# Gated block attention with a Fourier mixer on one core: the keys of nine head pairs turned by DMA transposes instead of TensorE

## The chip, the cores and the metric

The kernel runs on one core of a Trainium2 chip. The metric is the device time of one execution in microseconds (us). The engines are named as the profile names them: PE (TensorE), DVE (VectorE), ACT (ScalarE), POOL (GpSimd) and SP (SyncE, which here only issues DMAs).

## The reference

Inputs q, k and v have 4 batches, 8 heads, 768 positions and 64 dimensions. The output has 4 x 768 x 512 elements in float32.

```python
# attention: every query sees its own block of 64 keys and the three blocks with the best gate
k_rep  = k.reshape(B, H, 12, 64, D).mean(axis=3)
gate   = einsum('bhsd,bhnd->bhsn', q, k_rep)          # blocks ahead of the query's own: -1e9
mask   = (block in top 3 of gate, or own block) and key <= query
attn   = softmax(where(mask, q @ k.T / 8, -1e9)) @ v
x      = attn, heads side by side                     # (4, 768, 512)
# mixer and perceptron
u  = x + real(fft(fft(x, axis=1), axis=2))
un = (u - mean(u)) / sqrt(var(u) + 1e-6)
out = u + relu(un @ w_ch1) @ w_ch2                    # w_ch1 512 x 2048, w_ch2 2048 x 512
```

## The kernel before

The work is cut into 16 head pairs P (batch b = P // 4, two heads each), and for each batch into a Fourier step and a perceptron. Every step is a small function with a two-letter name, and a string `ORDER` lists all steps as `name:arguments`. Each engine, SP and POOL included, takes its own instructions in the order of that string; semaphores do the rest. So the order is fixed in advance, and it interleaves the perceptron of one batch with the attention of the next.

The steps of one pair:

- `Lk`, `Lq`, `Lv`: loads of keys, queries and values as they stand in memory (position on the partition), issued by SP (`load`, lines 270 and 275).
- `tk`, `tq`: six TensorE transposes each, of 128 x 128 float32, to put the dimension on the partition (line 292).
- `ks`: DVE sums the turned keys over each block of 64 (line 297); `kh` halves the result by head.
- `kc`: ACT copies the turned keys from PSUM into the tile `qk` in float16 (line 308, or 311 in two halves). `qc` and `qs` do the same for the queries by DVE and POOL.
- `g`, `gt`, `gx`, `gl`, `gm`: gate scores on PE, then transposes, top three and the mask on DVE. `K` (POOL, eight small selects) writes the mask into rows 64 to 95 of `qk`.
- `s`: six tiles of scores on PE, `e`: their exponentials on ACT, `d`: the causal select on POOL, `vc`: the cast of v on POOL, `v`: scores times v on PE, `x`: division on DVE.

The first seven pairs (P < `NX` = 7) add the mask by extra matmuls. The last nine pairs hold it inside the product: `qk` has 96 rows, 64 of the dimension and 32 that pair the mask on the query side with a 0/1 table of blocks (`ind`) on the key side. That table is loaded once into each of the three `qk` slots (`Lc`, `Li`).

For a batch: `fs`, `fd`, `f` (folds on DVE), `y` and `m` (Fourier products on PE), `ty`/`tr` (copies by ACT/DVE), `u` (DVE), `xu` (ACT), `un` (turn of the normalized input: for batch 0 by PE and DVE, for the others six DMA transposes of 128 x 512 float16 issued by SP, line 593), `w` (16 tiles of the first product, lines 629 and 631), `r` (relu on ACT or DVE), `c` (second product, lines 656 and 648), `o` (DVE, line 668), `od` (store, SP). `W` and `X` are the weights' casting loads, issued by POOL.

All PSUM tiles come from one pool of four buffers.

Of the kernel before, what the change touches and what calls it, by code (L numbers as in the profile page):

```python
# [11 lines left out]
FP = mybir.dt.float32  # L12
F16 = mybir.dt.float16
# [15 lines left out]
def _consts_np():  # L29
# [35 lines left out]
    ind = np.zeros((2, 32, S), np.float32)  # L65
    for e in range(2):
        ind[e, 16 * e:16 * e + NB] = nn[:, None] == (s[None, :] // 64)
# [5 lines left out]
                ind=ind.transpose(1, 0, 2).copy().astype(np.float16))  # L73
# [39 lines left out]
Lk:1 Lq:1 Lk:2 Lq:2 tk:0 ks:0 tq:0 Lq:3 Lk:3 kh:0 qc:0 iz:1 tk:1 qs:0 kc:0 g:0 ks:1 iz:0 gt:0 tq:1  # L113
kc:1 gx:0 Lq:4 Lv:0 Lk:4 Lv:1 kh:1 gl:0,0 tk:2 gl:0,1 gm:0 kc:2 qc:1 s:0,3 s:0,2 ks:2 e:0,3 qs:1
tq:2 Lq:5 Lk:5 s:0,5 qc:2 g:1 e:0,5 e:0,2 kh:2 s:0,4 gt:1 qs:2 s:0,0 e:0,4 gx:1 s:0,1 d:0,2 tq:3
gl:1,0 e:0,0 gl:1,1 tk:3 gm:1 e:0,1 d:0,0 qc:3 g:2 d:0,3 kc:3 d:0,5 s:1,5 gt:2 d:0,4 s:1,0 e:1,5
qs:3 ks:3 s:1,4 e:1,0 tq:4 d:0,1 gx:2 vc:0 e:1,4 s:1,3 qc:4 s:1,1 Lv:2 e:1,3 s:1,2 gl:2,0 kh:3
tk:4 gl:2,1 e:1,2 d:1,3 gm:2 g:3 d:1,4 ks:4 d:1,0 v:0 d:1,5 gt:3 vc:1 kc:4 gx:3 e:1,1 s:2,5 Lv:3
Lq:6 LF:0 Lq:7 Lk:6 Lk:7 LT:0 s:2,3 kh:4 gl:3,0 e:2,5 gl:3,1 s:2,4 e:2,3 d:1,1 x:0 tq:5 qs:4 e:2,4
g:4 d:2,3 gm:3 qc:5 s:2,0 d:2,4 s:2,2 d:1,2 e:2,0 gt:4 d:2,5 tk:5 vc:2 gx:4 e:2,2 s:2,1 ks:5 d:2,0  # L120
Lv:4 Lq:8 Lk:8 s:3,1 e:2,1 v:1 gl:4,0 kh:5 gl:4,1 kc:5 d:2,1 gm:4 d:2,2 s:3,2 x:1 e:3,1 vc:3 g:5
e:3,2 Lv:5 Lc:0 d:3,1 s:3,5 gt:5 s:3,0 fs:0,1 e:3,5 s:3,3 d:3,2 gx:5 e:3,0 s:3,4 fs:1,1 tq:6
gl:5,0 e:3,3 fs:0,0 v:2 gl:5,1 fs:1,0 e:3,4 d:3,3 qc:6 d:3,0 s:4,5 x:2 d:3,4 s:4,4 e:4,5 d:3,5
s:4,0 qs:5 v:3 e:4,0 gm:5 fs:2,0 fs:2,1 e:4,4 s:5,5 x:3 s:4,1 e:5,5 s:5,1 e:4,1 fd:2,0 s:4,2 s:5,0
fs:3,1 e:5,1 fs:3,0 s:5,2 fd:2,1 e:5,0 fd:3,1 s:4,3 fd:3,0 e:5,2 tk:6 f:0,1 f:0,2 e:4,3 Lk:9 Lq:9
tk:7 f:0,3 e:4,2 f:0,0 y:0,1 ks:7 pg:0 W:0 kc:6 y:0,0 tr:0,1 d:4,0 kc:7 d:4,4 d:4,5 ks:6 d:5,5
d:4,1 ty:0,1 tr:0,0 s:5,3 d:5,2 s:5,4 d:4,3 kh:6 W:1 ty:0,0 m:0,2 qs:6 e:5,3 u:0,2 m:0,1 vc:4
e:5,4 m:0,0 u:0,1 xu:0,2 d:5,4 tk:8 d:5,1 d:4,2 u:0,0 xu:0,1 d:5,0 xt:0,2 W:2 g:6 un:0,2 xu:0,0
xt:0,1 gt:6 tq:8 un:0,1 kc:8 xt:0,0 qc:8 tq:7 un:0,0 qs:8 v:4 Lq:10 Lk:10 Lv:6 Lq:11 qc:7 bn:0,3
w:0,4 d:5,3 qs:7 bn:0,1 w:0,5 r:0,4 gx:6 ks:8 w:0,6 r:0,5 gl:6,0 kh:7 gl:6,1 x:4 w:0,7 r:0,6 gm:6  # L130
w:0,3 r:0,7 s:6,5 r:0,3 s:6,1 e:6,5 s:6,3 e:6,1 kh:8 s:6,2 fs:4,0 bn:0,4 w:0,2 e:6,2 d:6,1 X:0
e:6,3 g:7 w:0,0 d:6,5 gt:7 r:0,2 d:6,3 vc:6 gx:7 s:6,4 r:0,0 vc:5 s:6,0 e:6,4 tk:9 Li:0 gl:7,0
Lv:7 tq:9 gl:7,1 e:6,0 gm:7 w:0,11 Lq:12 Lv:8 K:7 qc:9 kc:9 g:8 r:0,11 v:5 gt:8 d:6,0 ks:9 w:0,8
qs:9 gx:8 w:0,10 x:5 r:0,8 d:6,4 d:6,2 gl:8,0 s:7,5 s:7,2 r:0,10 kh:9 fs:4,1 w:0,1 bn:0,5 e:7,5
vc:7 e:7,2 tq:10 gl:8,1 Lv:9 r:0,1 X:1 gm:8 s:7,4 qc:10 w:0,15 d:7,2 e:7,4 K:8 bn:0,0 g:9 r:0,15
s:7,0 w:0,9 gt:9 e:7,0 gx:9 vc:8 tq:11 r:0,9 d:7,0 Lv:10 s:7,1 qc:11 d:7,5 tk:10 d:7,4 e:7,1
gl:9,0 s:7,3 ks:10 v:6 e:7,3 kh:10 gl:9,1 kc:10 gm:9 d:7,3 s:8,4 bn:0,2 d:7,1 w:0,12 vc:9 x:6
e:8,4 K:9 Lv:11 Lk:11 Lq:13 Lq:14 Lk:12 Lk:13 v:7 r:0,12 g:10 x:7 s:8,3 w:0,13 e:8,3 gt:10 nv:0
s:9,4 r:0,13 fs:5,1 s:9,1 fs:7,0 vc:11 w:0,14 e:9,4 fs:6,1 e:9,1 fs:7,1 s:8,1 fs:6,0 fs:5,0
c:0,2,0 r:0,14 fd:7,1 fd:6,1 e:8,1 gx:10 s:9,0 fd:7,0 s:9,2 e:9,0 fd:6,0 s:8,2 gl:10,0 c:0,3,0  # L140
f:1,3 e:9,2 f:1,2 e:8,2 gl:10,1 f:1,0 s:8,0 gm:10 s:9,3 d:8,2 e:8,0 y:1,1 d:8,1 d:9,0 e:9,3 nr:0
c:0,0,0 tr:1,1 ty:1,1 s:9,5 c:0,2,1 e:9,5 d:8,0 d:9,3 tk:11 K:10 s:8,5 c:0,1,0 Lk:14 ks:11 kc:11
c:0,3,1 f:1,1 d:9,5 e:8,5 d:9,1 qs:10 tq:12 o:0,2 y:1,0 od:0,2 kh:11 d:8,4 o:0,3 pg:1 vc:10 qc:12
c:0,1,1 od:0,3 ty:1,0 d:9,4 Lv:12 Lv:13 qs:11 tr:1,0 g:11 c:0,0,1 gt:11 d:8,3 d:8,5 gx:11 qs:12
m:1,0 o:0,0 m:1,1 od:0,0 o:0,1 d:9,2 od:0,1 v:8 u:1,1 m:1,2 u:1,0 xu:1,1 c:0,4,0 gl:11,0 xu:1,0
un:1,1 x:8 s:10,3 gl:11,1 un:1,0 c:0,4,1 u:1,2 e:10,3 d:10,3 fs:8,0 s:10,5 s:10,2 bn:1,3 e:10,5
tk:12 e:10,2 fs:8,1 v:9 gm:11 Lk:15 Lq:15 ks:12 xu:1,2 K:11 bn:1,0 tq:13 kc:12 un:1,2 c:0,5,0
qc:13 vc:13 bn:1,4 s:11,2 d:10,5 x:9 s:11,4 vc:12 e:11,2 c:0,5,1 bn:1,1 Lv:14 Lv:15 e:11,4 s:11,0
# [12 lines left out]
e:13,3 c:1,1,1 un:2,0 d:13,3 d:13,2 s:14,5 v:12 o:1,0 kh:15 od:1,0 o:1,1 v:13 e:14,5 bn:2,1 od:1,1
d:14,5 x:12 qs:15 s:14,3 m:2,2 e:14,3 bn:2,0 c:1,4,0 x:13 fs:13,0 g:15 fs:13,1 c:1,5,0 u:2,2
fs:12,0 xu:2,2 gt:15 c:1,2,0 bn:2,4 un:2,2 gx:15 c:1,5,1 gl:15,0 fs:12,1 gl:15,1 gm:15 bn:2,5
c:1,4,1 K:15 c:1,2,1 o:1,4 od:1,4 o:1,5 s:14,1 od:1,5 s:15,4 e:14,1 s:15,0 c:1,3,0 e:15,4 d:14,1
d:14,3 e:15,0 d:15,4 s:14,4 s:14,2 d:15,0 e:14,4 s:15,2 c:1,3,1 e:15,2 e:14,2 s:15,3 o:1,3 w:2,1
od:1,3 o:1,2 bn:2,2 w:2,2 od:1,2 r:2,1 s:15,5 w:2,4 e:15,5 w:2,15 r:2,4 r:2,2 w:2,3 r:2,15 e:15,3
s:15,1 r:2,3 d:15,3 w:2,9 d:14,4 e:15,1 d:14,2 d:15,2 d:15,5 s:14,0 r:2,9 d:15,1 w:2,14 e:14,0
v:15 d:14,0 w:2,5 x:15 w:2,7 r:2,5 fs:15,1 fs:15,0 r:2,14 fd:15,1 v:14 fd:15,0 r:2,7 w:2,6 x:14
w:2,11 fs:14,0 fs:14,1 fd:14,1 w:2,13 fd:14,0 f:3,2 f:3,0 w:2,10 r:2,13 r:2,11 w:2,8 f:3,3 r:2,10
f:3,1 nv:2 w:2,0 r:2,8 nr:2 r:2,6 y:3,1 r:2,0 y:3,0 ty:3,1 c:2,0,0 pg:3 tr:3,0 tr:3,1 w:2,12  # L170
c:2,1,0 r:2,12 ty:3,0 c:2,0,1 c:2,1,1 m:3,0 o:2,0 c:2,2,0 od:2,0 u:3,0 o:2,1 xu:3,0 m:3,1 od:2,1
c:2,4,0 u:3,1 un:3,0 xu:3,1 bn:3,2 m:3,2 c:2,3,0 u:3,2 un:3,1 bn:3,3 xu:3,2 c:2,5,0 bn:3,0 un:3,2
# [613 lines left out]
```

## Time and profile before

| | |
|---|---|
| runs shown | 297.56 us median of 3 (297.54 to 297.93) |
| span of the profiled execution, first to last instruction | 295.6 us |
| what lies around it, by the median | 297.56 - 295.6 = 1.96 us |
| granted TensorE clock | 1.000 |
| ACT busy, share of the span | 164.2 us, 56% |
| POOL busy, share of the span | 111.1 us, 38% |
| DMA queues | 93200 packets, 33.53 MB |

The profile comes from one execution, and its span is set against the runs' median by adding what lies around it. Matmuls are pipelined, so an instruction's duration is longer than the time that it adds to PE's stream; the latter is read from the distance between starts, which the chain of waits shows as the length of its pieces.

### The profile page before, as it was taken

Reading aid. Unit: us, or ns where it says so; the run is one execution under the profiler, and the core shown is the slowest. Engines: PE = TensorE matmul, PEld = TensorE weight load, DVE = VectorE, ACT = ScalarE, POOL = GpSimd, SP = SyncE. Lnnn points to the kernel's source line nnn. Section 1 sums busy time; section 2 is a strip of 40 time slices with the busy share of each in tenths; the row PEclk is TensorE's granted clock in tenths of the full one; section 3 lists DMA queues with packets and bytes.
Section 4 is the critical chain, followed back from the end, with each engine's and each line's share of the span. In section 5 each row is a group of like instructions: output and inputs, shape, how many; then the busy total and the mean of one; then the engine's idle time right before and its main releaser. Section 6 shows DMA issues by size and latency. Waiting matters only on the chain.

```text
span 295.6 us, 6738 instructions
## 1 busy us (share of the span) xinstructions
PE 286.5 (97%) x2633; PEld 180.2 (61%) x2633; DVE 192.5 (65%) x597; ACT 164.2 (56%) x205; POOL 111.1 (38%) x286
## 2 busy tenths in 40 slices
PE   8899999999999999999999999999999999999995
PEld 4566767765676556656757667446666554555453
DVE  2999999986988638987796577714493282700132
ACT  3698989749578841677788843165524250155000
POOL 2267528528776289064753363220303000110000
PEclk9999999999999999999999999999999999999999
DMA  8999999997999727477000005311000052300023
GB/s 197 268 228 230 262 245 199 195 230 118 226 185 211 168 55 186 118 164 176 3 0 2 0 9 136 38 72 71 2 1 2 32 103 44 142 0 2 0 91 125
DMA packets 93200, 33.53 MB, mean 113 GB/s; under 512 B 85936, under 2 KB 89968, under 8 KB 93168
## 3 DMA queue, kind: packets, MB, share of 16 engines
q1 hardware_dynamic: 87504, 28.47, 40.6%
q0 software_dynamic: 3664, 4.19, 9.1%
q10 hardware_dynamic: 2000, 0.44, 0.7%
q8 instruction: 21, 0.34, 0.5%
q14 instruction: 11, 0.09, 0.1%
HBM read 28.63 MB, written 6.29 MB: 118 GB/s over the span
## 4 chain that ended last, share of the span: by engine, by line
PE 84%; DVE 7%; ACT 6%; DMA 1%; issue 1%; DVEq 0%; ACTq 0%
PE c L656 26%; PE h L629 19%; PE h L631 10%; PE sc L414 7%; PE av L449 6%; ACT pt L431 5%; PE tp L292 5%; PE yp L519 2%; PE mx L552 2%; DVE q L316 2%; PE mx L553 1%; PE warmps L693 1%; DVE u L566 1%; PE g L342 1%; PE c L648 1%; PE sc L409 1%
## 5 line engine op out<-in xcount | busy, mean ns | idle before, releaser
L431 ACT ACTIVATE pt<-sc 128x1024 f16<-128x1024 f32 (+1 forms) x96 | 83.3, 923 | 26.6 <-PE sc L414 19.7
L629 PE MATMUL h<-unT,w 128*128 128x512 f16 x256 | 85.1, 379 | 0.0
L656 PE MATMUL c<-w_sb,hT 128*128 128x512 f16 x368 | 83.8, 379 | 0.0
L631 PE MATMUL h<-unT,w 128*128 128x256 f16 x256 | 69.7, 272 | 0.4 <-DMA unT<-x 0.4
L641 ACT ACTIVATE hT<-h 128x768 f16<-128x768 f32 x48 | 37.8, 813 | 43.7 <-PE h L631 43.7
L656 PEld LDWEIGHTS <-hT 128*128 128x128 f16 x368 | 35.6, 98 | 39.3 <-issue 0.5
L437 POOL TENSOR_SCALAR_AFFINE_SELECT pt<-pt 128x256 f16<-128x256 f16 x96 | 37.5, 414 | 58.5 <-ACT pt L431 57.6
L629 PEld LDWEIGHTS <-w 128*128 128x128 f16 x256 | 25.0, 97 | 29.2 <-issue 1.3
L668 DVE SCALAR_TENSOR_TENSOR u<-c,rs,u 128x512 f32<-128x512 f32 (+1 forms) x25 | 17.5, 725 | 31.2 <-PE c L656 30.4
L639 DVE TENSOR_SCALAR hT<-h 128x768 f16<-128x768 f32 x16 | 15.3, 955 | 29.7 <-PE h L631 29.6
L578 ACT ACTIVATE x<-u,nm 128x512 f16<-128x512 f32 x24 | 15.9, 715 | 22.5 <-DVE nm L572 22.3
L292 PE MATMUL tp<-id,nat 128*128 128x128 f32 x192 | 27.5, 284 | 0.6 <-ACT pt L431 0.3
L631 PEld LDWEIGHTS <-w 128*128 128x128 f16 x256 | 25.0, 98 | 4.3
L225 POOL TENSOR_SCALAR_AFFINE_SELECT qk<-mt 32x160 f16<-32x160 f16 x72 | 23.1, 341 | 10.8 <-DVE mt L386 9.1
L414 PE MATMUL sc<-qk 96*128 96x512 f16 (+3 forms) x144 | 26.8, 305 | 0.0
L225 POOL TENSOR_SCALAR_AFFINE_SELECT qk<-q 64x768 f16<-64x768 f32 (+1 forms) x25 | 20.6, 825 | 14.8 <-DVE q L316 14.1
L292 PEld LDWEIGHTS tp<-id,nat 128*128 128x128 f32 x192 | 22.2, 146 | 5.7 <-issue 1.6
L449 PE MATMUL av<-v,pt 128*128 128x65 f16 x672 | 23.0, 193 | 0.1
L449 PEld LDWEIGHTS <-pt 128*128 128x128 f16 x672 | 22.0, 97 | 1.7 <-POOL pt L437 0.5
L297 DVE TENSOR_REDUCE kr<-tp 128x12 f32<-128x768 f32 x16 | 15.1, 945 | 5.9 <-PE tp L292 5.9
L222 POOL TENSOR_TENSOR t<-vr,rs 128x6 f32<-128x6 f32 x12 | 2.4, 199 | 43.5 <-DVE rs L609 42.9
L414 PEld LDWEIGHTS <-qk 96*128 96x128 f16 x144 | 13.3, 97 | 8.9 <-issue 0.5
(95 smaller groups left out, 351.2 us busy)
## 6 DMA issues: line engine op xcount, KB each, us to landing
nat<-in_v_dram SPq DMA_DIRECT2D x16, 384.0 KB, 4.7
nat<-in_k_dram SPq DMA_DIRECT2D x31, 192.0 KB, 3.5
nat<-in_q_dram SPq DMA_DIRECT2D x31, 192.0 KB, 3.9
out_dram<-u SPq DMA_DIRECT2D x23, 256.0 KB, 2.1
w_sb<-in_moe_w_ch_dram POOLq DMA_DIRECT2D x2, 1024.0 KB, 10.2
w<-in_moe_w_ch_dram POOLq DMA_DIRECT2D x2, 768.0 KB, 8.4
fs_sb<-c_FS SPq DMA_DIRECT2D x1, 582.0 KB, 5.1
w<-in_moe_w_ch_dram POOLq DMA_DIRECT2D x1, 512.0 KB, 7.3
```

What stands on the lines that cost most here:

```text
L225: nc.gpsimd.affine_select(out=out, in_=in_, pattern=[[0, i] for i in n], base=0, channel_multiplier=0, compare_op=ALU.is_ge, fill=0.0)
L292: nc.tensor.transpose(ps[:, 128 * st:128 * st + 128], src[:, st, :], id32)
L414: nc.tensor.matmul(ps[:, e, co:co + q1 - q0], qk[0:96, e, 1, 128 * jt:128 * jt + 128], qk[0:96, e, 0, q0:q1], start=True, stop=True)
L431: nc.scalar.activation(out=d["pt"][:, o:o + 2 * n].rearrange("p (e c) -> p e c", e=2), in_=d["sc", i][:, :, 0:n], func=AF.Exp, scale=0.125)
L437: nc.gpsimd.affine_select(out=dg, in_=dg, pattern=[[0, 2], [1, 128]], base=0, channel_multiplier=-1, compare_op=ALU.is_ge, fill=0.0)
L449: nc.tensor.matmul(av[:, e, 66 * st:66 * st + 65], pt[:, co:co + 128], vv[:, e, jt, 0:65], start=(cnt == 0), stop=(cnt == 20))
L578: nc.scalar.activation(out=x_b[:, 2 * kp + k2, :], in_=u_b[:, k2, :], func=AF.Identity, scale=0.0625, bias=nm[:, k2:k2 + 1])
L629: nc.tensor.matmul(hp[:, 0:512], w1s, unT[:, dt, 0:512], start=(dt == 0), stop=(dt == NDT - 1))
L631: nc.tensor.matmul(hp[:, 512:768], w1s, unT[:, dt, 512:768], start=(dt == 0), stop=(dt == NDT - 1))
L641: nc.scalar.activation(out=hT, in_=hp, func=AF.Relu)
L656: nc.tensor.matmul(c_ps[b, g[0]][:, st - g[0], :], h_t[b, it][:, 128 * st:128 * (st + 1)], w2_sb[:, it, :], start=(it == 0), stop=(it == N ...
L668: nc.vector.scalar_tensor_tensor(out=o, in0=ps, scalar=st_t[b][1][:, st:st + 1], in1=o, op0=ALU.mult, op1=ALU.add)
```

## The change

For the last nine pairs the keys no longer pass through PE and ACT.

- `La` (new, POOL): a casting load of the pair's keys into the first 64 columns of each 128-column block of a float16 tile `k16n` (two buffers). The other 64 columns hold the 0/1 table of blocks, loaded once (`Lc`).
- `kt` (new, SP): two DMA transposes of 128 x 768 float16 from `k16n` into the slot of `qk`, which bring keys and table rows together. `qk` is indexed side first, head second.
- `Lk` for these pairs loads the keys a second time, eight positions to a partition (96 partitions), into one buffer `ksrc`; `ka` (new, DVE) sums each eight of them.
- `tk` for these pairs is one small float32 matmul that adds the eights to blocks of 64, into columns of the PSUM tile that also takes the gate scores. `ks` and `kc` are gone for them; `kh` reads PSUM.
- The loads of the first seven pairs' keys use `ksrc` and the two `k16n` tiles in turn, in place of three buffers of their own. `Li` is gone.
- `ORDER` is new as a whole.

```diff
+    ksrc = ctile([128, 1024], FP, "ksrc")
+    k16n = [ctile([128, 2, NST, 128], F16, f"k16n{i}") for i in range(2)]
+    row8 = ctile([96, NB], FP, "row8")
...
+        if who == 1 and P >= NX:
+            eng.dma_start(ksrc[0:96].rearrange("p (e r) -> p e r", e=2),
+                          src[b, 2 * hp:2 * hp + 2].rearrange("e (p r) d -> p e (r d)", r=8))
+            return
...
+    def k_load(P):
+        b, hp = divmod(P, NP)
+        nc.gpsimd.dma_start(out=k16n[P % 2].rearrange("p e st d -> p (e st) d")[:, :, 0:64],
+                            in_=k[b, 2 * hp:2 * hp + 2].rearrange("e (st p) d -> p (e st) d", p=128))
+
+    def k_add(P):
+        x = ksrc[0:96].rearrange("p (e r) -> p e r", e=2)
+        pairs[P]["k8"] = k8 = spool.tile([96, 128], FP, tag="k8", name=f"k8_{P}", bufs=2)
+        nc.vector.tensor_reduce(out=k8.rearrange("p (e d) -> p e d", e=2),
+                                in_=x.rearrange("p e (r d) -> p e d r", d=64),
+                                axis=mybir.AxisListType.X, op=ALU.add)
+
+    def k_turn(P):
+        for e in range(2):
+            nc.sync.dma_start_transpose(qk_s[P % NSLOT][:, 1, e, :]
+                                        .rearrange("p (st c) -> p st c", c=128),
+                                        k16n[P % 2][:, e].rearrange("p st d -> p (st d)"))
+
+    def k_blocks(P):
+        d = pairs[P]
+        d["slot"] = P % NSLOT
+        d["g"] = g = pst([128, 172], f"g_{P}")
+        nc.tensor.matmul(g[:, 160:172], d["k8"], row8, start=True, stop=True)
...
-        if P < NX:
-            nc.scalar.copy(out=qk[:, 1, XW(P), :], in_=ps)
-        else:
-            for e in range(2):
-                nc.scalar.copy(out=qk[0:64, e, 1, :], in_=ps[64 * e:64 * e + 64])
+        nc.scalar.copy(out=qk[:, 1, XW(P), :], in_=ps)
...
-                pcopy(qk[0:64, e, 0, :], q32[64 * e:64 * e + 64], [S])
+                pcopy(qk[0:64, 0, e, :], q32[64 * e:64 * e + 64], [S])
...
-        for i in range(1, NSLOT):
-            nc.sync.dma_start(qk_s[i][64:96, :, 1, :], dr["ind"].ap())
+        nc.sync.dma_start(row8, dr["row8"].ap())
+        for t in k16n:
+            nc.sync.dma_start(t[:, :, :, 64:128].rearrange("p e st d -> p (e st) d"),
+                              dr["ind"].ap().rearrange("p (x d) -> p x d", d=64))
```

Seven lines of the new order, around pairs 7 to 10 (each engine picks out its own steps):

```
w:0,1 e:6,0 tq:9 qc:9 e:6,3 ka:9 qs:8 d:5,1 d:5,3 d:5,4 d:5,5 La:8 d:6,4 vc:5 qs:7 d:6,2 La:9 d:5,2
X:0 d:6,3 d:6,5 K:7 d:6,0 qs:9 vc:6 d:6,1 s:7,5 r:0,10 v:5 x:5 s:7,2 s:7,3 r:0,0 w:0,15 r:0,1 e:7,5
s:7,0 e:7,2 r:0,15 s:7,4 tq:10 e:7,3 bn:0,2 gl:8,0 e:7,0 e:7,4 w:0,8 r:0,8 tk:9 w:0,9 v:6 kh:9 s:7,1
r:0,9 qc:10 g:9 gl:8,1 w:0,13 e:7,1 gm:8 Lk:10 kt:8 X:1 d:7,2 d:7,3 d:7,5 vc:7 K:8 La:10 d:7,4 d:7,1
d:7,0 s:8,1 e:8,1 s:8,2 w:0,14 r:0,13 bn:0,4 r:0,14 nv:0 x:6 v:7 s:8,3 e:8,3 c:0,2,0 w:0,12 gt:9
e:8,2 fs:5,1 gx:9 fs:6,1 fs:6,0 ka:10 x:7 tk:10 tq:11 fs:4,0 fd:6,1 fd:6,0 gl:9,0 gl:9,1 gm:9 d:8,1
nr:0 K:9 Lk:11 kt:9 Lv:8 qc:11 r:0,12 kh:10 c:0,3,0 g:10 s:9,2 ka:11 fs:7,0 fs:7,1 fs:5,0 fd:7,1
```

## The prediction

> **What bounds the kernel now.** I read the busy times and the shares of the chain first, then busy time by stage (cut at the start of the first `w`, at 58.6 us), then pieces of the chain, then groups.
>
> ```profile
> span 295.6 us, 6738 instructions
> PE 286.5 (97%) x2633; PEld 180.2 (61%) x2633; DVE 192.5 (65%) x597; ACT 164.2 (56%) x205; POOL 111.1 (38%) x286
> PE 84%; DVE 7%; ACT 6%; DMA 1%; issue 1%; DVEq 0%; ACTq 0%
> ```
>
> ```profile
> core 0: us, PE busy (x) PEld busy (x) DVE busy (x) ACT busy (x) POOL busy (x), PEclk, DMA share, GB/s
> 0.00:58.60 58.60, 53.30 (x749) 38.24 (x750) 50.77 (x170) 47.18 (x59) 28.65 (x70) 1.00 1.05 228
> 58.60:100.00 41.40, 41.40 (x423) 26.34 (x420) 35.12 (x137) 29.34 (x36) 24.14 (x53) 1.00 1.02 199
> 100.00:200.00 100.00, 99.62 (x857) 62.07 (x856) 68.72 (x213) 59.84 (x75) 50.73 (x132) 1.00 0.32 74
> 200.00:295.60 95.60, 92.13 (x614) 53.51 (x611) 37.93 (x81) 27.87 (x37) 7.53 (x32) 1.00 0.16 48
> ```
>
> There are two regimes. From 58.6 us PE is never idle but for 0.4 us and the tail, at full clock: it is the bound, and whatever leaves its stream is worth its full time. Before that, DVE (50.8 of 58.6) and ACT (47.2) form the chain. The DMA engines are full until 100 us (shares 1.05 and 1.02), then mostly free. Pieces of the chain (start, length, what):
>
> ```profile
> 54.52 0.60 DVE unT L590
> 58.76 0.22 PE h L629
> 79.81 0.66 PE tp L292 x6
> 82.20 0.41 PE g L342 x8
> ```
>
> ```profile
> L292 PE MATMUL tp<-id,nat 128*128 128x128 f32 x192 | 27.5, 284 | 0.6 <-ACT pt L431 0.3
> L297 DVE TENSOR_REDUCE kr<-tp 128x12 f32<-128x768 f32 x16 | 15.1, 945 | 5.9 <-PE tp L292 5.9
> L311 ACT CAST qk<-tp 64x768 f16<-64x768 f32 x18 | 14.3, 792 | 3.2 <-DVE kr L297 3.1
> ```
>
> The trap is in the second group of lines: a transpose lasts 284 ns, so six look like 1.7 us, but six take 0.66 us of PE's stream (79.81 to 80.46). DVE's last copy into `unT` lets the first `w` go.
>
> **PE's stream.** By distances between starts, the nine turns that go (pairs 7 to 15) take 0.91, 0.71, 0.71, 0.66, 0.66, 0.66, 0.71, 0.66 and 0.66 us: 6.34 us. The first two (1.62) lie ahead of the first `w`, where PE isn't the bound; seven (4.72) come off the bound. Added are nine small float32 matmuls, all behind the first `w`. Nearest rows: four gate matmuls are eight records in 0.41 us, so one matmul of two records at least 0.10; two turns of 128 weights would be 0.22. I take 0.15, so 1.35. Net on the bound -3.4 us (-3.8 to -2.7).
>
> **The first stage.** Ahead of the first `w` DVE loses two sums (`ks:7`, `ks:8`, 0.95 each, 1.9 us) and ACT four half copies (3.2 us). In the old chain `ks:7` stands between the two `tr`, and `kc:7` ahead of `ty`. Pairs 0 to 6 otherwise do the same work. Gain between 0 and 3.2; I take 1.5, a little under DVE's share, as the chain also passes through PE. The first `w` then starts at 57.0.
>
> **Work that others cover.** ACT's 18 copies (18 x 0.79 = 14.3 us) earn nothing behind 58.6 us, where PE hides them. DVE's `ka` reads 1024 elements to a partition where `ks` read 768: 0.945 x 1024/768 = 1.26 us, so +2.8 us in all, covered where DVE is 69 to 85% busy; without cover up to 0.3 a pair. POOL issues nine more casting loads; the five in the trace took 757 to 954 ns, so about 9 us on an engine 38% busy. The tightest is `La:9`, queued ahead of `d:5,2`, for which `v:5` waits: done near 69.7, due 74.1, 4 us spare. The step `tk` holds a PSUM buffer from the small matmul to `gt`, some 4 to 6 us, in place of the turn's own.
>
> DMA work: by packet records (18 ns for 256 B, 86 ns for 2 KB, 16 engines) each pair loses a load of 1536 small packets (1.7 us of all engines) and gains a casting one of as many rows (1.7), 192 long packets (1.0) and 1536 packets of transposes (1.7): +2.8 us, of which four pairs fall in the full stretch before 100 us. Loads there run about 13 us ahead (`Lq:8` landed at 42, PE used it at 55), which is the cover.
>
> **The new waits.** What the trace shows of a DMA transpose, for 128 x 512:
>
> ```profile
> L593 SPq DMA_TRANSPOSE unT<-x x18: 1196/1217/1927, 120.5 to 244.9; - x18
> DMA to landing us min/median/max: 2.4/2.5/4.1
> ```
>
> So SP needs 1.2 us to issue one and it lands 1.25 us after that. For 128 x 768 I take 1.8 and 1.25: a `kt` of two lands 4.9 us after its start. The first group below is for `nat` loads between 66 and 92 us, while the two `w_sb` loads fly, the second for 100 to 116 us:
>
> ```profile
> DMA to landing us min/median/max: 4.0/5.1/7.1
> ```
>
> ```profile
> DMA to landing us min/median/max: 2.5/3.4/5.0
> ```
>
> Between 66 and 92 us a landing can be 4 us later, and `kt:8` and `kt:9` fall there. I laid PE's steps out in the new order at the paces of the trace (`w` 1.30, `c` 1.73, `v` 1.28, `s` 0.43, turn 0.66, `g` 0.41), from 57.0. Of the old order this leaves 1.9 us unexplained after 58.6; I leave the same in the new one. Then, step by step:
> - `s:8` is due at 85.3. In SP's queue `kt:8` stands behind `Lk:10`, which waits for `ka:9`, which DVE takes after `qc:9`; the turn `tq:9` ends at 74.1, so 74.1 + 0.95 + 1.26 = 76.3, and keys by 81.2, or 85 if loaded. On time, just.
> - `s:9` is due at 95.1. `g:9` ends at 84.0; DVE then does `gt`, `fs`, `gx` (1.5), two `fs` and `ka:10`, to 88.3; `Lk:11` and `kt:9` follow, keys by 93.5, loaded 97. `K:9` waits for `gm:9` (after `x:7`, `fs`, `fd`; 92.1) and needs eight selects of 0.34: 94.9. Late by 0 to 2.
> - `y:1,1` is due at 105.6; DVE's queue reaches the end of `f:1,3` at about 106.6. Late by 1.
> - `s:13` is due at 144.7. `kt:13` stands behind `Lk:15`, that behind `ka:14`, that behind `r:1,11` (`w:1,11` ends at 136.2): issued from 138.7, keys by 143.6. On time by 1, and the DMA is quiet there.
> - `kt:10`, `11`, `12`, `14` and `15` have 7 us or more. Queued behind them on SP are `Lv`, `Lq`, `od` and `un:1`; `un:1` lands near 124, `w:1` is due at 130.5.
>
> A late PE also gives later steps time, so these don't add up in full. I take +2.0 us, between 0 and 9.
>
> **Sum.** -3.4 - 1.5 + 2.0 = -2.9 us: the span goes from 295.6 to 292.7, and with 1.96 us around it the time from 297.56 to about 294.7 us.
>
> **Rivals.**
> 1. *The transposes come late* (slower). Place: `s:8`, `s:9`, then `s:13`. If a transpose beside `w_sb` loads is delayed as the `nat` loads are and SP's queue carries it on, each of pairs 8 and 9 is 3 us late and 13 is 2: +8 in place of +2.0, 300.7 us. It decides from 4.9 us of lateness. For it: DMA share 1.02 there, and +2.8 us a pair. Against: loads run far ahead, and PE waited 0.4 us for DMA in all.
> 2. *DVE and POOL set the pace between 84 and 106 us* (`ka`, `gx`, `K`, folds in one queue): +4 in place of +2.0, 296.7 us, near no change. For it: DVE 35.1 of 41.4 us busy. Against: DVE sat at 85% before too and PE didn't wait.
> 3. *The small matmul costs as much as the six turns*, so the change doesn't relieve PE: 9 x 0.66 in place of 1.35, 299.3 us. Against it: a twelve-column product against 768 columns.
> 4. *No lateness, full gain ahead*: -3.8 - 3.2 = -7.0, 290.5 us.
> 5. *The casting loads' descriptors are held up by DVE.* If POOL had to wait out two DVE operations of 0.95 us (the row of L297) with each `La`, that is 1.9 us a pair; most have 8 us spare, so what remains is `La:9` with `d:5,2` and the queue behind it: up to +1.9, 296.6 us. Against it: the five casting loads in the trace took 757 to 954 ns to issue, with DVE 79 to 99% busy around them. The Trainium skill speaks against the change here (SBUF — State Buffer, section "SBUF: two separate sides"): GpSimd writes the descriptors of its DMAs through a port that some DVE modes hold, and a load of about 620 ns took about 3100. By those figures I would estimate 2.5 us for each load and 297.2 us; the trace doesn't bear it out.
>
> **How the numbers follow.** The forecast (291.5 to 296.2, by lateness of 0 to 3.5 us and the bounds of the other two terms): 0.48. Rival 1 0.22, rival 2 0.16, rival 3 0.04, rival 4 0.05, rival 5 0.05. A measurement here can tell 0.2%, 0.6 us: faster is below 296.96, slower above 298.16. Faster: 0.48 + 0.05 + 0.05 of rival 2 + 0.02 of rival 5 = 0.60. Same: 0.05 of rival 2 + 0.02 of rival 5 = 0.07. Slower: the rest, 0.33. The range runs from 291.0, which leaves out most of rival 4, to 300.5, which leaves out about half of rival 1.
>
> **What would show it.** Right: the first `w` at 56 to 58 us; the pieces of `g` for pairs 7 to 15 unchanged and the small matmul at 0.10 to 0.22 us; PE idle behind the first `w` under 3 us, most of it ahead of `s:9` and `y:1,1`; DMA transposes of 1.8 us on SP. Wrong: PE waits for `qk` from a DMA or POOL by more than 5 us in sum, a `kt` that lands 8 us after its start, or a first `w` later than 58.6.

## The result, and the profile after

The changed kernel takes 319.61 us (median of 4 runs, 317.6 to 320.98) against 297.61 us for the kernel before on the same chip: a ratio of 1.073 (95% interval 1.069 to 1.078). The forecast was 294.7. In the later runs the medians of the kernel before were 297.5 to 298.1 us. Single executions of a kernel can be slower than the rest, and the profiled ones of `e6`, `e8` and `e11` lay 7, 3 and 25 us above their medians, so medians and ratios are compared, and these three profiles are read only for what waited for what, for the first `w` and for when DMAs were issued and landed.

The page of the changed kernel, with the lines that answer to the first ones of before (its profiled execution took 317.6 us):

```profile
span 315.9 us, 6672 instructions
PE 286.2 (91%) x2597; PEld 177.2 (56%) x2597; DVE 204.7 (65%) x597; ACT 151.2 (48%) x187; POOL 120.9 (38%) x295
PE 57%; DVE 19%; DMA 10%; ACT 7%; POOL 2%; issue 2%; SPq 1%; ACTq 0%; DVEq 0%
```

PE's share of the chain fell from 84 to 57%, and DMA's rose from 1 to 10%. By stage, cut at the first `w` (now at 62.5 us; same columns as before):

```profile
0.00:62.50 62.50, 50.95 (x737) 37.06 (x738) 50.83 (x174) 44.18 (x55) 27.93 (x65) 1.00 1.17 205
62.50:100.00 37.50, 31.33 (x310) 19.45 (x309) 31.11 (x95) 17.66 (x22) 23.05 (x46) 0.98 1.19 183
100.00:200.00 100.00, 94.54 (x812) 58.25 (x811) 75.56 (x214) 53.48 (x66) 55.41 (x137) 0.97 0.76 128
200.00:316.00 116.00, 109.38 (x743) 62.48 (x740) 47.18 (x117) 35.84 (x46) 14.55 (x48) 1.00 0.19 55
```

PE, which was never idle from 58.6 to 100 us, is now idle for 6.2 us of 37.5 between the first `w` and 100 us. The DMA share stays high up to about 140 us.

I used one ledger for all runs: for each of PE's steps in order, the distance from its start to the next step's start, less the lower quartile of that distance for the same kind of step in the trace of before (for the small matmul, 0.15). The sum is what PE lost. Before: first `w` at 58.6 us, 2.0 us lost behind it. After: first `w` at 62.5 (+3.9), 21.7 lost (+19.7). The last step of PE starts 20.4 us later, so its stream did become 3.2 us shorter. The largest losses are 4.6 us at `s:8` and 2.6 between `s:10,4` and `c:0,5,0`; eight more are between 0.9 and 1.4.

PE's two longest waits between 62 and 110 us, and what POOL's casting load waited for (us in total, times, longest):

```profile
PE sc L453 <- DMA qk<-k16n: 4.2, 1, 4.2
PE g L335 <- DVE k L321: 1.1, 1, 1.1
```

```profile
POOL k16n L315 <- DMA qk<-k16n: 5.3, 1, 5.3
```

And all that SP issued between 84 and 98.3 us (start, length, what):

```profile
85.75 0.33 SPq L290 DMA_DIRECT2D ksrc<-in_k_dram  x1
86.20 2.73 SPq L327 DMA_TRANSPOSE qk<-k16n  x2
97.83 0.32 SPq L290 DMA_DIRECT2D ksrc<-in_k_dram  x1
98.25 2.54 SPq L327 DMA_TRANSPOSE qk<-k16n  x2
```

These are `Lk:10`, `kt:8`, `Lk:11`, `kt:9`. `kt:9` had its source since 81.9 us (`La:9` landed) and was issued at 98.25, because it stands behind `Lk:11`, which waits for `ka:10` to free the one buffer `ksrc`. I call this the round of the buffer: a load `Lk`, the sum `ka` that reads it, then the next load.

### The profile page after: what moved, and what is told of

It reads as the page before. It is cut to its first block, busy times and chain, and to the rows that moved or that the text cites. A ratio compares the mean times of both kernels' runs of the same rounds, so it can differ in the third digit from the quotient of the medians.

```text
span 315.9 us, 6672 instructions
## 1 busy us (share of the span) xinstructions
PE 286.2 (91%) x2597; PEld 177.2 (56%) x2597; DVE 204.7 (65%) x597; ACT 151.2 (48%) x187; POOL 120.9 (38%) x295
## 4 chain that ended last, share of the span: by engine, by line
PE 57%; DVE 19%; DMA 10%; ACT 7%; POOL 2%; issue 2%; SPq 1%; ACTq 0%; DVEq 0%
PE c L695 24%; PE h L668 12%; PE h L670 6%; DMA ksrc<-in_k_dram 5%; ACT pt L470 4%; PE sc L453 4%; DMA qk<-k16n 4%; PE av L488 3%; DVE k L321 2%; DVE q L355 2%; DVE mx L405 2%; DMA indc<-c_indc 2%; PE yp L558 2%; DVE u L605 2%; PE mx L591 1%
## 5 line engine op out<-in xcount | busy, mean ns | idle before, releaser
L695 PE MATMUL c<-w_sb,hT 128*128 128x512 f16 x368 | 85.1, 383 | 3.3 <-DVE u L707 3.3
L668 PEld LDWEIGHTS <-w 128*128 128x128 f16 x256 | 25.5, 100 | 29.3 <-issue 1.9
L670 PEld LDWEIGHTS <-w 128*128 128x128 f16 x256 | 25.2, 98 | 5.8 <-issue 2.1
L617 ACT ACTIVATE x<-u,nm 128x512 f16<-128x512 f32 x24 | 16.0, 714 | 16.4 <-DVE nm L611 8.2
L227 POOL TENSOR_SCALAR_AFFINE_SELECT v<-nat 128x768 f16<-128x768 f32 x16 | 15.0, 938 | 21.6 <-PE h L670 13.6
L321 DVE TENSOR_REDUCE k<-ksrc 96x128 f32<-96x1024 f32 x9 | 17.5, 1940 | 6.1 <-DMA ksrc<-in_k_dram 6.1
L605 DVE SCALAR_TENSOR_TENSOR u<-mx,x 128x512 f32<-128x512 f32 x24 | 15.6, 687 | 6.5 <-PE mx L592 6.5
L448 PE MATMUL sc<-qk 64*128 64x512 f16 (+3 forms) x112 | 14.8, 305 | 3.4 <-ACT qk L350 1.6
## 6 DMA issues: line engine op xcount, KB each, us to landing
w_sb<-in_moe_w_ch_dram POOLq DMA_DIRECT2D x2, 1024.0 KB, 12.1
```

The source lines that it names most:

```text
L227: nc.gpsimd.affine_select(out=out, in_=in_, pattern=[[0, i] for i in n], base=0, channel_multiplier=0, compare_op=ALU.is_ge, fill=0.0)
L321: nc.vector.tensor_reduce(out=k8.rearrange("p (e d) -> p e d", e=2), in_=x.rearrange("p e (r d) -> p e d r", d=64), axis=mybir.AxisListTyp ...
L605: nc.vector.scalar_tensor_tensor(out=u_b[:, k2, :].rearrange("p (m two) -> p two m", two=2), in0=mps[:, k2, :].rearrange("p (two m) -> p t ...
L668: nc.tensor.matmul(hp[:, 0:512], w1s, unT[:, dt, 0:512], start=(dt == 0), stop=(dt == NDT - 1))
L670: nc.tensor.matmul(hp[:, 512:768], w1s, unT[:, dt, 512:768], start=(dt == 0), stop=(dt == NDT - 1))
L695: nc.tensor.matmul(c_ps[b, g[0]][:, st - g[0], :], h_t[b, it][:, 128 * st:128 * (st + 1)], w2_sb[:, it, :], start=(it == 0), stop=(it == N ...
```

## The experiments

Where the first four texts name theories by letters, A says that the place of the load tiles in SBUF makes the packets slow, B that the amount and order of the work does; C says that DVE's longer sum `ka` feeds the lateness, D that DVE has slack there.

**Placement.** The row loads write 256 B to a partition row. In packet records between 5 and 20 us they took 18 ns before and 25 ns after. Before, `nat0` and `nat1` lay at multiples of 512 B and `nat2` 128 B beyond one; after, these and the tiles in their place lay 64 B further on.

`e1_pad64`: 64 B ahead of `ksrc`, so that all lie at multiples of 128.

```
+    pad = ctile([128, 16], FP, "pad")
     ksrc = ctile([128, 1024], FP, "ksrc")
```

> The changed kernel with 64 bytes put ahead of ksrc, so that ksrc, k16n, nat0 and nat2 begin at multiples of 128 bytes in a partition, as the nat tiles of before did (in the changed kernel they begin 64 beyond one). Theory A, the place: between 5 and 20 us the 256-byte load packets took 25 ns in the changed kernel and 18 before, with the same loads in flight, because each row now crosses a 128-byte line. It expects 18 ns again, a load of 192 KB every 0.67 us instead of 0.9, the first w at 57 to 59 us instead of 62.5, and 305 to 312 us in place of 319.6, since the full DMA stretch after it eases too. Theory B, the amount and order of the work: the packets are slow because of what is in flight together. It expects 25 ns still and 317 to 321 us.

319.15 us, 1.072 (1.067 to 1.077); packets still 25 ns. A multiple of 128 is not enough, so the 128-byte line that theory A names is not what counts.

`e2_before_pad64`: the same 64 B in the kernel before, ahead of `v_s`, so that its load tiles lie 64 B on.

> The kernel before with 64 bytes put ahead of v16, which moves its nat tiles from multiples of 128 bytes to 64 beyond. Theory A expects 25 ns packets, the first w 3 to 5 us later than 58.6, and 300 to 305 us. Theory B expects no change: 297.3 to 297.9 us.

299.69 us against 297.96, 1.0105 (1.003 to 1.018; three of its four runs lie between 299.3 and 299.8, one at 303.9); packets 25 ns, and the first `w` at 60.6 us instead of 58.6. Placement alone slows the loads of a kernel that is otherwise unchanged, and costs it some 2 us.

`e3_all_aligned`: `lim` moved behind `row8`, then the pad; `ksrc`, `k16n`, `qk` and the weights at multiples of 512, `nat0` at 128 and `nat2` at 256 beyond one.

```
-    lim = ctile([128, 4, 4], FP, "lim")
...
     row8 = ctile([96, NB], FP, "row8")
+    lim = ctile([128, 4, 4], FP, "lim")
+    pad = ctile([128, 16], FP, "pad")
```

> As the changed kernel with 64 bytes of padding, and with a small tile moved so that the weights' tiles and qk, where the transposes and the casting loads of the weights land, begin at multiples of 512 bytes instead of 64 beyond. Theory A carried further (every DMA destination suffers) expects 1 to 4 us less than with the padding alone. Theory A for 256-byte rows alone, and theory B, expect the time of the padding alone within 1 us.

316.52 us, 1.063 (1.060 to 1.065); packets 18 to 19 ns. Placement is worth about 3 of the 22 us. `nat0` and `nat2` lie here as in `e1`; only the other tiles moved, and the packets were fast. All later kernels but `e4` are built on this one.

**The sum.** `e4_adds`: on `e1`, `ka` as three additions of contiguous halves.

```
-        nc.vector.tensor_reduce(out=k8..., in_=x..., axis=mybir.AxisListType.X, op=ALU.add)
+        for n in (256, 128):
+            tt(x[:, :, 0:n], x[:, :, 0:n], x[:, :, n:2 * n], ALU.add)
+        tt(k8..., x[:, :, 0:64], x[:, :, 64:128], ALU.add)
```

> The changed kernel with 64 bytes of padding, and the sum over eight positions as three additions of contiguous halves (512, 256 and 128 elements) in place of one reduction with a step of 64. The reduction took 1940 ns where 1260 had been reckoned. Theory C, DVE's longer sum feeds the lateness through SP's queue (the second load of keys waits for it, and kt waits behind that): each sum falls to about 1.1 us, and the time by 2 to 5 us against the padding alone. Theory D, DVE has slack there: under 1 us.

319.39 us, 1.070: no gain, since the three additions take 0.75 + 0.62 + 0.44 = 1.81 us where the sum took 1.94. Theory C expected sums of 1.1 us, so this run doesn't decide between C and D.

**The first stage.** In the changed kernel's chain (start, length, what):

```profile
2.10 5.58 DMA indc<-c_indc
7.71 0.83 ACT indz L751
8.54 0.71 ACT qk L350
9.27 0.97 DVE kr L340
```

The new order has `kc:0` ahead of `ks:0` and `iz:1` ahead of both on ACT. `ks:0` reads the PSUM tile that `kc:0` reads, so it waited for that copy, which stood behind `iz:1`, which waits for a small constant. `g:0` starts at 11.5 us; before, where `ks:0` came first, it started at 8.9.

`e5_sums_first`: only this turned round.

```
-... tk:0 iz:1 kc:0 iz:0 tq:0 ks:0 kh:0 qc:0 tk:1 ...
+... tk:0 ks:0 tq:0 kh:0 qc:0 kc:0 iz:1 iz:0 tk:1 ...
```

> The kernel with all tiles aligned (316.52 us, first w at 62.0 us), and one edit: pair 0's block sums (ks:0) and its q steps stand ahead of kc:0 and iz:1 in the order, as they did in the kernel before. If kc:0 ahead of ks:0 is what delays the first gate product (ks:0 waited for ACT's copy from the same PSUM tile, and that copy for iz:1, which waits for the indc load): g:0 about 1.6 us earlier, first w at 60.0 to 60.8, time 314.5 to 315.5. If the first stage is set by something else (POOL's selects, loads): first w within 0.5 us of 62.0, time 316 to 317.3.

315.12 us, 1.056 (1.047 to 1.064; the interval takes in the 1.063 of `e3`, so a gain in time isn't shown). `g:0` at 8.6 us, but the first `w` at 61.3: of 1.9 us won at `g:0` against `e3`, 0.8 arrive there. The rest of the lateness is elsewhere in the remade first stage.

**The transposes' place.** `e6_turns_first`, on `e3`:

```
-... Lk:10 kt:8 ... Lk:11 kt:9 ... Lk:12 kt:10 ... Lk:15 kt:13 kt:14
+... La:8 kt:8 ... La:9 kt:9 ... Lk:10 ... kt:10 Lk:11 ... kt:13 Lk:15 kt:14
```

> The kernel with all tiles aligned, and one edit: kt:8, kt:9, kt:10 and kt:13 are issued on SP ahead of the key load that waits for ka (kt:8 behind La:8, kt:9 behind La:9, kt:10 ahead of Lk:11, kt:13 ahead of Lk:15). Everything else is as it was. If the transposes' place in SP's queue behind the single buffer of keys is the main cause: s:8 at 86 to 89 us (91.6), s:9 at 95 to 102 (109.5), y:1 at least 6 us earlier, time 304 to 310. If it is DVE's and POOL's queues (ka, the selects, K) that hold pairs 8 and 9: s:9 still at 106 or later, time 313 to 317. If the transposes are slow wherever they fly, s:8 moves by under 1 us.

316.61 us, 1.063 (1.061 to 1.066): nothing gained. The wait had moved. `kt:8` and `kt:9` were issued 7 to 11 us earlier than in `e3`, beside the two `w_sb` loads, and landed after 8.8 to 15.8 us. Now `Lk:10` stood behind them on SP (issued 90.75, landed 104.4), so `ka:10` waited, and behind it on DVE stood `x`, for which PE waited 9 us. My theory that the transposes' place is the main cause fell.

`e7_old_start`: `e6`, with the order of before up to the first `w`, without the steps that are gone, and with `Lk:7` and `La:7` put in.

> The transposes first as in e6, and up to the first w the order of the kernel before with only the removed steps taken out (ks, kc and tk of pairs 7 and 8) and Lk:7 and La:7 put in; from the first w on the changed kernel's order. If the remade order of the first stage is what costs it time: first w at 57 to 59.5 us (62.0 with the remade order), and 2 to 4 us less than e6. If the load rows and the method set it: first w at 61 to 62.5 and the time of e6 within 1 us.

The first `w` came at 59.0 us (63.3 in `e6`), and the time was 320.7 us, 1.077 (1.073 to 1.080). `Lk:8`, behind `kt:7` on SP, was issued at 72.25 instead of 66.2, and PE waited 6.4 us ahead of `tk:8`. More than the time won was lost, most of it at the next step that hangs on `ksrc`.

`e8_both`: `e5` and `e6` together.

> The edits of e5 and e6 together. If the two causes are independent, the gains add to within 1 us (302 to 309). If time won ahead of the first w is lost again at the transposes of pairs 8 and 9, the time is that of e6.

317.89 us, 1.060 (1.053 to 1.067; single runs from 313.9 to 321.3). The first `w` came at 61.4, and PE lost the same 9 us at the same step as in `e6`. The interval takes in the ratios of both `e5` and `e6`, so it isn't shown whether what `e5` won in the first stage survives.

**Pairs 10 to 15 alone.** `e9_from_ten` gives pairs 7 to 9 their keys through PE as before (with the old key layout, and `e3`'s placement), in the order of before with the new steps put in by hand.

```
+    NK = 10
-        if who == 1 and P >= NX:
+        if who == 1 and P >= NK:
...
-        "tk": lambda P: k_blocks(P) if P >= NX else a_tp(P, 1), ...
+        "tk": lambda P: k_blocks(P) if P >= NK else a_tp(P, 1), ...
```

> The new way (casting load, transposes, ka, small matmul) only for pairs 10 to 15; pairs 7, 8 and 9 take their keys through PE as before, in the order of the kernel before, into which the steps of the new way are put by hand. The new way then starts where the DMA engines are no longer full (about 100 us). If the loss comes from pairs 7 to 9 in the full stretch and from the remade order: first w at 58 to 59.5, PE saves 6 x (0.68 - 0.15) = 3.2 us, time 293.5 to 297. If the way itself is slow wherever it stands (ka on DVE, the wait for the small matmul, SP's queue): PE idle behind 100 us by several us, time 299 to 306.

300.32 us, 1.0097 (1.007 to 1.013); first `w` at 58.6, 7.5 us lost behind it. Nearly all of the 22 us is gone, so it lies in pairs 7 to 9 and the remade order, which this run takes away together. From pair 10 on the way still costs some 3 us more than it saves, as the second of the two expectations had it.

**The weight loads.** `e10_turns_less_w` (on `e6`) and `e11_less_w` (on `e3`) load one eighth of `w_sb`.

```
-    nc.gpsimd.dma_start(out=w2_sb[:, 8 * c:8 * (c + 1), :], in_=moe_w_ch2[1024 * c:1024 * (c + 1), :]...)
+    nc.gpsimd.dma_start(out=w2_sb[:, 8 * c, :], in_=moe_w_ch2[1024 * c:1024 * c + 128, :])
...
-                             w2_sb[:, it, :], start=(it == 0), ...
+                             w2_sb[:, it - it % 8, :], start=(it == 0), ...
```

> e6 (transposes of pairs 8, 9, 10 and 13 first) with seven eighths of the two w_sb loads left out: each loads 128 of its 1024 rows, and the second MoE product reads these for all (so its output isn't the reference's; PE's work is the same). If the transposes, the casting loads and Lk:10 were held up by the w_sb loads that fly beside them: the kt of pairs 8 and 9 land 2.5 to 6 us after their issue (8.8 to 15.8 in e6), Lk:10 within 5 us (13.7), the 9 us of PE behind c:0,2,0 shrink to under 3, time 303 to 309. If they are slow for another reason (the transposes block their own queue, SP issues slowly): landings of 8 us or more stay, time 313 or more.

> The aligned kernel (changed kernel's order) with the same seven eighths of the w_sb loads left out (so not the reference's output). If the w_sb loads beside the transposes are the cause of the lateness of s:8: kt:8 lands within 4 us, PE loses under 3 us at s:8,1 (6.5), but kt still stands behind Lk:10 and La:10 behind kt:8: time 308 to 312. If the place behind the single key buffer alone is the cause: s:8 loses 5 us or more and the time is 314 to 317.

313.28 us (1.052) and 312.87 us (1.048): 3.3 and some 4 us less than with the full loads. In `e10` the transposes of `kt:8` landed after 8.5 and 5.2 us, those of `kt:9` after 2.5 and 3.5 and `Lk:10` after 3.9, and still PE lost 16.4 us: `Lk:11` stood behind `kt:10`, which waited for `La:10`. In `e11` `kt:8`, with its place in the queue unchanged, landed after 5.4 and 4.7 us, where it took 7.6 and 11.2 in the changed kernel and 4.5 and 13.2 in `e3`. The loads make it worse; they aren't the main cause.

**The round of the one buffer.** `e13_one_load`: `e6` without `Lk:8` to `Lk:15`; `e14_neither`: with the cut of `w_sb` as well.

```
-... Lk:8 ... Lk:9 ... Lk:10 ... Lk:11 ... Lk:12 ... Lk:13 ... Lk:14 ... Lk:15
```

> e6 (transposes first, aligned tiles) with the key loads Lk:8 to Lk:15 left out: the block sums of pairs 8 to 15 are taken from pair 7's rows (so the output isn't the reference's), by the same ka, small matmul and transposes. SP then never waits for ka, and 3 MB less is loaded. If the single buffer (load, ka, next load) is what costs pairs 8 to 11: PE loses under 14 us behind the first w (27 in e6), time 302 to 308. If the transposes beside the w_sb loads are: transposes still land 8 us or more after issue, time 310 to 315.

> e13 with seven eighths of the w_sb loads left out too (not the reference's output). If the single buffer and the w_sb loads are the two causes behind the first w: PE loses under 9 us, time 298 to 303, what is left being the first stage (first w at 62 to 63 us instead of 58.6). If something else costs as much (ka and DVE, POOL's K): PE loses over 12 us, time 305 or more.

307.15 us, 1.033 (1.029 to 1.037), and 307.53 us, 1.034 (1.030 to 1.037). PE's waits between 62 and 110 us in `e13`, all of them:

```profile
PE h L669 <- DVE x L224: 0.2, 1, 0.2
```

The changed kernel's waits of 4.2 us for a DMA and 1.1 for a sum have no counterpart here, and the time is 9.5 us below that of `e6`, with the transposes still beside the `w_sb` loads (landing 2.5 to 7.5 us after issue). The round is worth 9.5 us with the `w_sb` loads (`e6` to `e13`) and 5.8 without (`e10` to `e14`); the `w_sb` loads cost 3.3 us with the round and nothing without it. So the two prices overlap. `e13` also spares eight loads of 384 KB; that these alone would bring 9.5 us is unlikely by `e14`, where a further 1.8 MB less brought none, and by `e10`, where the transposes landed about as soon and the time was 6.1 us longer. But no run kept the loads and took the round away, and none had a second buffer. In `e14` PE still lost 12.1 us behind the first `w`: something else costs as much, as the second expectation had it.

`e18_one_load_old_start`: `e13` with the start of `e7`.

> e13 (Lk:8 to Lk:15 left out, so not the reference's output; 307.15 us) with the start of e7 (the order of the kernel before up to the first w). If the first stage adds to the rest: first w at 58.8 to 59.5, 3 to 4 us less than e13, 303 to 304.5. If a gain there is lost again behind it: 305.5 to 307.5.

311.09 us, 1.046 (1.044 to 1.048): slower than `e13`, with the first `w` at 58.7. What PE waited for, and what stood in POOL's queue:

```profile
POOL k16n L316 <- DMA qk<-k16n: 5.0, 1, 5.0
PE sc L454 <- POOL qk L227: 4.3, 1, 4.3
```

`La:9` refills the `k16n` buffer that `kt:7` reads, so POOL waited 5.0 us for `kt:7` to land, and `K:7` stood behind it. PE lost 4.5 us there: the four us won ahead were given back at the next shared buffer, and some 2 to 4 more were lost elsewhere.

**Does the way pay where the DMA is free?** `e12_from_ten_order` moved ten entries of the order of `e9` (`ka:12` behind `x:9`, `ka:13` behind `gt:12`, and what hangs on them).

> e9 (new way for pairs 10 to 15 alone; 300.3 us, PE lost 7.5 us behind the first w, where the kernel before lost 2.0) with eight steps moved: ka:12 behind x:9 and ka:13 behind gt:12 on DVE, their small matmuls and key loads with them, c:0,1,1 ahead of y:1,0, kh:10 ahead of x:6, the indicator loads 15 us later on SP. If e9's losses are only places in the queues: PE loses 3 to 5 us, time 295.5 to 298. If ka's 1.94 us on a DVE that has little to spare sets it wherever it stands: 299 to 301.

309.14 us, 1.038: it had put `Lk:13` ahead of `ka:12`, so that pair 12's sums read pair 13's rows and `ka:12` waited 8.1 us for that load, which SP issued only behind the four transposes of `un:1,2` and `kt:12`. PE lost 8.1 us ahead of its small matmul. An accident, but it prices one late turn of the round at about 9 us.

`e15_sum_after_xu` and `e16_sum_after_x` put that right, with `ka:12` at two places.

Against `e9`, first `e15`, then `e16` (the other moved steps, told in the text on record, are common to both):

```
-... gl:11,1 ka:12 un:1,0 ... Lk:13 Lq:15 ... xu:1,2 K:11 ... x:9 ka:13 ... gt:12 ...
+... gl:11,1 un:1,0 ... Lq:15 ... xu:1,2 ka:12 Lk:13 K:11 ... x:9 ... gt:12 ka:13 ...
```

```
-... gl:11,1 ka:12 un:1,0 ... Lk:13 Lq:15 ... xu:1,2 K:11 ... x:9 ka:13 ... gt:12 ...
+... gl:11,1 un:1,0 ... Lq:15 ... xu:1,2 K:11 ... x:9 ka:12 Lk:13 ... gt:12 ka:13 ...
```

> e9 with steps moved, and with Lk:13 behind ka:12 (in e12 it stood ahead of ka:12, so that pair 12's sums read pair 13's rows): ka:12 and Lk:13 behind xu:1,2, tk:12 behind c:0,5,1, ka:13 behind gt:12, tk:13 behind w:1,0, Lk:14 behind kt:13, kh:10 ahead of x:6, c:0,1,1 ahead of y:1,0, the indicator loads behind Lq:14. If e9's losses are places in the queues: PE loses 3.5 to 5.5 us behind the first w (7.5 in e9), time 296 to 298.5. If they come from ka's 1.94 us wherever it stands: 299.5 to 301.

> The same with ka:12 and Lk:13 some 4 us later (behind x:9) and tk:12 behind s:11,0. If DVE's queue ahead of w:1 is what ka:12 holds up: 0.5 to 1.5 us less than with ka:12 behind xu:1,2. If the round of load, sum and load through one buffer is already the tighter: PE waits at tk:12 or tk:13, 1 to 4 us more.

299.68 us, 1.006 (1.004 to 1.009), and 298.89 us, 1.005 (1.003 to 1.007). By the intervals the two can't be told apart. In `e16` PE waited 2.0 us for `ka:13`: `Lk:13` had been issued 2.9 us after `ka:12` ended, behind `kt:12`.

`e17_load13_first`: `e16` with the load ahead of the transposes, and `tk:13` and `kh:13` a little later.

```
-... un:1,2 kt:12 ... x:9 ka:12 Lk:13 ... w:1,0 tk:13 ... kh:13 ... s:10,4
+... un:1,2 ... x:9 ka:12 Lk:13 kt:12 ... w:1,0 ... s:10,4 tk:13 ... kh:13 gx:12
```

> As e16 (ka:12 behind x:9), but Lk:13 ahead of kt:12 in SP's queue, where it stood behind it and was issued 2.9 us after ka:12 was done, and tk:13 and kh:13 two steps later (behind s:10,4 and ahead of gx:12). If the round through the key buffer is what e16 lost at tk:13 (2.1 us): that loss is gone, time 296.8 to 298.2, level with the kernel before or a little better. If the way costs as much elsewhere again: 298.5 to 300.

297.25 us, 0.999 (0.997 to 1.001). Its page, and its stages from the first `w` of before:

```profile
span 296.2 us, 6715 instructions
PE 71%; DVE 11%; ACT 5%; DMA 4%; issue 4%; POOL 2%; DVEq 0%; POOLq 0%; ACTq 0%
```

```profile
58.60:100.00 41.40, 40.69 (x416) 25.75 (x413) 34.74 (x131) 27.51 (x33) 26.08 (x55) 1.00 1.06 195
100.00:200.00 100.00, 98.40 (x836) 59.41 (x834) 73.20 (x219) 51.44 (x66) 55.53 (x136) 1.00 0.66 116
```

PE loses 4.8 us behind the first `w` (2.0 before) and its stream is about 3 us shorter: nothing is left over. With every step of the round in time the way is level with the kernel before, not ahead of it, and no version here beats it by what a measurement can tell.

## Why the prediction was wrong

**PE's stream** was right: a small matmul (two records) takes 0.143 us of it by the median (0.14 to 0.24) where I took 0.15, and the stream became 3.2 us shorter by the ledger where I had 3.4. That six transposes are worth their 0.66 us of stream, and not the 1.7 of their records, was borne out.

**The first stage** was wrong in sign: +3.9 us in place of -1.5. I counted the sums and copies taken away and assumed that the rest of the stage kept its pace. The new order changed the pace: with the old one, and the sums and copies still gone, the first `w` comes at 59.0 and 58.7 us (`e7`, `e18`), so even then nothing of the 1.5 appears. Placement, which I didn't look at, adds to it (2.0 us in `e2`).

**Work that others cover** was under-sized. `ka` lasts 1.94 us, not 1.26:

```profile
L321 DVE TENSOR_REDUCE k<-ksrc 96x128 f32<-96x1024 f32 x9 | 17.5, 1940 | 6.1 <-DMA ksrc<-in_k_dram 6.1
```

I had scaled the sum over PSUM by its elements. The packets of the casting loads took 32 ns where I took 18 for any 256 B read: 13824 of them are 28.0 us of 16 engines, not 15.6. The transposes were the one thing over-sized: issued in 1.2 us, not 1.8.

**The new waits** hold the step that failed: the lateness of +2.0 us, between 0 and 9, was 19.7 by the ledger. I named the right place (`s:8`) and the right queue, and found `s:8` on time, from a first `w` at 57.0. PE reached it at 94.3 in place of 85.3, 5.5 us late from the first stage and 3.5 from losses behind it, and then waited 4.2. I had reckoned `ka:9` from the end of `tq:9` at 74.1 and `kt:8` from 76.3; `kt:8` was issued at 86.2. Of these ten us some 8 are PE's own lateness at `tq:9`; the others are the wait of `ka:9` for its rows (0.6), its longer sum (0.7) and the issue of `Lk:10` ahead (0.4). As PE was as late as `kt:8`, what made it wait is the landing. I took 8.7 us from the start of a loaded `kt` to its landing, and it took 12.5: its second transpose landed 11.2 us after its issue, 0.3 us after the `w_sb` load that was issued with it (98.7 and 98.4). With the landing as I priced it PE would have waited less than half a us.

```profile
87.48 11.20 DMA qk<-k16n
```

The round of the buffer I hadn't priced at all. `Lk:9` waits for `ka:8`, which waits for `Lk:8`. The trace of after gives `Lk:8` issued 65.6 and landed 74.4, `ka:8` to 76.3 (PE waited 1.1 us for it at `tk:8`), `Lk:9` to 83.7, `ka:9` to 85.7, `Lk:10` and only then `kt:8`. With one buffer each pair needs a whole round of load (3.3 to 8.7 us), sum (1.9) and DVE's queue ahead of it; I priced the sum alone. The lateness then feeds itself. `ka:10` stood on DVE behind 10 us of other work with hardly a gap (it started at 95.9, though `Lk:10` had landed at 89.5), and `Lk:11` and `kt:9` behind `ka:10`. PE waited at `s:8`, so `v:7` came late; on DVE `x:7` waited 6.1 us for it, and `ka:11`, behind `x:7`, started at 109.2, though `Lk:11` had landed at 101.2. PE came to `s:9` 15 us after its due time, but it did not wait there, as the keys had landed 5 us before: the 15 us are the 5.5 of the first stage and 9.6 lost ahead of `s:9`. It waited for the round again at `c:0,5,0`. `Lk:13` was issued only at 135.2, behind `un:1,0`; `ka:13` waited 3.6 us for it, `o:0,4` stands behind `ka:13` on DVE, and PE waited for `o:0,4`:

```profile
140.74 1.93 DVE L321 TENSOR_REDUCE k<-ksrc 96x128 f32<-96x1024 f32 x1 [3.60 <-DMA ksrc<-in_k_dram]
142.69 0.73 DVE L707 SCALAR_TENSOR_TENSOR u<-c,rs,u 128x512 f32<-128x512 f32 x1
143.47 3.30 PE L695 MATMUL c<-w_sb,hT 128*128 128x512 f16 x8 [2.39 <-DVE u L707]
```

The idle time then costs a second time, since behind each of these two waits the granted clock is half for 3.4 us (columns as above). The eight matmuls of `c:0,5,0` took 3.3 us instead of 1.73, and both stretches together cost some 3 us.

```profile
98.60:101.90 3.30, 3.17 (x10) 1.50 (x11) 0.00 (x0) 1.73 (x2) 2.60 (x6) 0.50 1.01 214
142.90:146.30 3.40, 2.83 (x7) 0.98 (x7) 0.52 (x1) 0.00 (x0) 0.12 (x1) 0.50 0.77 174
```

The Trainium skill has this (TensorE: Matmul & The Clock Gate, section "Part 1: The HAM clock gate (the "warmup" mystery)"): an array that idles for some 3.4 us drops to half clock. The trace agrees at `s:8`, where PE stood idle for 4.2 us; at `c:0,5,0` 2.4 us were enough. I had given a late PE no second price.

So of the 21.7 us lost, 4.2 are the wait at `s:8`, 1.3 and 2.6 the losses at `tk:8` and `c:0,5,0`, some 3 the half clock and 4.7 four waits of the remade order without a DMA (below); the rest is in smaller pieces.

**Rivals.** Rival 1 had the mechanism, a transpose that comes late and carries on through SP's queue, at a price of 8 us and a chance of 0.22; by the runs the round costs 5.8 to 9.5, besides what the order and the first stage cost. Its price was bounded by landings 4 us later, where `kt:8` took 3.8 more than that, and it held no round that waits for itself. Rival 2's reason against it (DVE at 85% and PE not waiting) failed with the new order: DVE's queue carried the lateness on, as at `c:0,5,0`. Rival 3 fell (0.143 us). Rival 5 fell too: `La` was issued in 1.03 to 1.10 us, not in the 2.5 estimated from the Trainium skill's figures (SBUF — State Buffer, section "SBUF: two separate sides"). POOL did stand still at `La:10`, but for a landing, because the transposes still read that buffer.

**The range** (291.0 to 300.5) left 319.6 far outside because every rival was one wait at the old pace; none put a slower first stage, a longer landing, the round and the half clock together. The stated 291.5 to 296.2 doesn't follow from its parts either: with the bounds of the other two terms it would be 290.6 to 298.4, and with those terms at their middle 292.7 to 296.2. Neither comes near 319.6. Of the three signs of being wrong that I had named, two came: a first `w` at 62.5 us and a `kt` that landed 12.5 us after its start. PE's waits for `qk` stayed under 5 us (4.2).

**What stays open.** `e13` still loses 10.7 us more than before behind the first `w`. Some of it stands in the profiles with the remade order, at the same steps and with no DMA near: 1.28 us twice, where PE waits for ACT's `pt` at `s:14` and `s:15`, and about 0.9 to 1.1 at `w:1,6` and `c:2,1,1`. Another 1.8 us is lost ahead of `g:11`, where `kh:11` stands behind folds in DVE's queue, and 1.6 in 3.4 us at half clock behind that. The other 4.5 of its 12.7 us, in smaller pieces, weren't taken apart. That aligned tiles give 3 us is shown; which tiles and which address bits count was not settled.

## What to carry to other kernels

A buffer of one is a loop: its period is the load's landing, the work that frees it, and whatever stands ahead of either in its queue, and everything queued behind the next load inherits that period. Date a step from the landing of its data back through the step that freed the buffer, not only from the engine that runs it, and take its landing from the longest beside the same loads. Moving one waiting DMA ahead of another on the same queue moves the wait (`e6`, `e7`); to see whether a loop is the cause, take the loop out. Don't count a step as free because its wait is short: a wait that lets the clock fall is paid twice.

## What the hardware showed

- Loads in rows of 256 B took 18 ns a packet in the kernel before and 25 ns with its tiles 64 B further on (`e2`), which cost it some 2 us of 298. In the changed kernel they took 25 ns, and still did with the tiles at multiples of 128 B (`e1`); in `e3`, with most of them at multiples of 512 B, 18 to 19 ns.
- A casting row (256 B read, 128 B written) took 32 ns.
- Behind a wait of PE of 4.2 us, and behind one of 2.4 us, the granted clock was 0.50 for 3.4 us.
- A DMA transpose of 128 x 768 is issued in 1.2 us and lands after 2.5 to 2.8 us in quiet, as one of 128 x 512 did before. Beside the casting `w_sb` loads `kt:8` landed after 7.6 and 11.2 us, and `w_sb` after 12.1 (10.2 before). All transposes of the changed kernel (issue, then landing; shortest, median, longest):

```profile
L327 SPq DMA_TRANSPOSE qk<-k16n x18: 1209/1237/4481, 52.0 to 202.4; - x18
DMA to landing us min/median/max: 2.7/3.9/13.7
```
